# One more FFT batch transposed through DRAM, half of a batch's low parts moved to GpSimd, and its last stage two iterations sooner

## The chip, the cores and the metric

The kernel runs on one core of a Trainium2 chip. The metric is the device time of one execution in microseconds (us): the median of the runs shown. Five engines work side by side, each through its own queue of instructions in order: PE (TensorE: matmuls; PEld is its weight load), DVE (VectorE), ACT (ScalarE), POOL (GpSimd) and SP (SyncE, which here only issues DMAs). ACT issues DMAs too.

## The reference

```python
X = np.fft.rfft(x, axis=1)                       # x: 8 batches of 3136 x 256, float32
y = np.fft.irfft(X * F, n=x.shape[1], axis=1)    # F = filt_r + 1j * filt_i
h = np.maximum(y @ w_in, 0.0)                    # w_in: 256 x 1024
conv_out = sum(conv_w[k] * shift(h, k) for k in range(3))
out = (h * gate(conv_out)) @ w_out               # gate: sigmoid; w_out: 1024 x 256
```

## The kernel before, in words

The FFT over 3136 = 112 x 28 is done with matmuls, in stages. For each of 8 batches there are 14 steps (p = 0 to 13) of each stage:

- `load` (L314) brings two columns of x, 224 KB, into one of XBUFS = 7 buffers; SP issues it.
- `first` (L319) is the transform of length 112 on PE. `keep` (L333) empties its PSUM tile on ACT. For most batches it goes into an SBUF tile `turn`, which `turn` (L347, PE transposes of L352) and `turned_rows` (L355, a copy on ACT, L357) later bring into the order of the next stage. For the batches in `THROUGH_DRAM` (L577: 2, 4 and 6) `first` has another shape (L325 instead of L330), ACT writes the result to `a_dram` (L337), and `load_rows` (L341) reads it back in the new order (L344), so that PE and ACT have no transposing to do.
- `second` (L361 to L368) is the transform of length 28 on PE; `filt` (L370) multiplies by the filter with three DVE operations (L376 to L378) and adds with one on POOL (L380), giving `z`.
- `third` (L231) is the first inverse stage on PE (L234); `store` (L236) copies it on ACT (L238) and ACT writes it to `b_dram` (L240).
- `last_load` (L197) reads `b_dram` back into one of four tiles `br`; `last_stage` (L210) is the last inverse stage, eight passes of PE in L216; `last_out` (L219) splits the result into y = high + low: ACT rounds to the high part (L146), DVE subtracts to get the low part (L149). Both write y with a stride.

A loop over iterations i (L404) runs these as a pipeline, one step of each stage in each iteration: `first` of step i-1, `turn` of step m = i-17, `second` of m-1, `filt` of m-2, `third` of m-4. It ends with i = 130. In the last iterations, from 113 (`done`), there is no `first` left; batch 7 goes through its later stages, and batch 0's last stage runs beside it: its load of piece c/2 is written in iteration 115 + c/2, its matmuls one iteration later and its `last_out` two later (`LATE` = 2 in L426).

Then the feed-forward network (FFN) starts, with m counting its pieces (L550): `inner` (L476, six matmuls in L177 to L179), `relu` and scaling on ACT, `conv` on DVE (L494, L495), sigmoid on ACT (L499), product on DVE (L500), a split of g into high (ACT) and low (POOL, L152), and `project` on PE (L520 to L522), six pieces later. The first `inner` reads y of batch 0 in all 28 columns, so it waits for the last `last_out`. The last three `third` of batch 7 and their `store` run in pieces 1 to 3 of the FFN. Batches 1 to 7 have their last stages inside the FFN.

The order of the work on PE, DVE, ACT and POOL is the order in which the code is written (`manual_schedule`, L403). SP is not among these: a scheduler orders its DMA issues, in which each waits for its buffer to be free. Tiles of `a` (ABUFS = 4 buffers) serve `keep`, `load_rows` and `turned_rows`.

In the profiled execution iteration 112 starts at 299.3 us, 113 at 302.0, 115 at 305.9 and 129 at 347.7; the FFN's first matmul starts at 353.8.

Of the kernel before, what the change touches and what calls it, by code (L numbers as in the profile page):

```python
# [9 lines left out]
F32 = mybir.dt.float32  # L10
# [3 lines left out]
AF = mybir.ActivationFunctionType  # L14
# [3 lines left out]
N1 = 112  # L18
N2 = 28
G = 28  # L20
D = 256
FF = 1024
KT = D // 128
# [101 lines left out]
def tile_fft_filter_gated_ffn(  # L125
# [16 lines left out]
    nc = tc.nc  # L142
    B = x.shape[0]

    def hi_act(dst, src):
        nc.scalar.activation(dst, src, AF.Copy)  # L146

    def lo_dve(dst, src, hi):
        nc.vector.tensor_tensor(out=dst, in0=src, in1=hi.bitcast(F32), op=ALU.subtract)  # L149

    def lo_pool(dst, src, hi):
        nc.gpsimd.tensor_tensor(out=dst, in0=src, in1=hi.bitcast(F32), op=ALU.subtract)  # L152

    def to_f32(dst, raw, e, m):


        v = nc.vector
        pairs = raw.rearrange("p (n t) -> p n t", t=2)
        low, high = pairs[:, :, 0].bitcast(U32), pairs[:, :, 1]
        v.tensor_scalar(e, high, 3, 0x3FFFFFF8, op0=ALU.logical_shift_left, op1=ALU.bitwise_and)  # L160
        yield
        v.tensor_scalar(m, high, 30, 30, op0=ALU.logical_shift_right, op1=ALU.logical_shift_left)
        yield
        v.tensor_tensor(out=e, in0=e, in1=m, op=ALU.bitwise_or)
        yield
        v.tensor_scalar(m, high, 27, 0xF, op0=ALU.logical_shift_right, op1=ALU.bitwise_and)
        yield
        v.scalar_tensor_tensor(out=dst, in0=m, scalar=7.0, in1=e.bitcast(F32), op0=ALU.is_ge, op1=ALU.mult)
        yield
        v.tensor_scalar(e, dst.bitcast(I32), 23, 23, op0=ALU.logical_shift_right, op1=ALU.logical_shift_left)  # L170
        yield
        v.scalar_tensor_tensor(out=e.bitcast(F32), in0=low, scalar=2.0**-52, in1=e.bitcast(F32), op0=ALU.mult, op1=ALU.mult)
        yield
        nc.gpsimd.tensor_tensor(out=dst, in0=dst, in1=e.bitcast(F32), op=ALU.add)
# [6 lines left out]
    dram = ctx.enter_context(tc.tile_pool(name="dram", bufs=1, space=bass.MemoryType.DRAM))  # L181
    a_dram = {b: dram.tile([N2, 112, D], F32, name=f"a_dram{b}") for b in THROUGH_DRAM}
    b_dram = [dram.tile([N2, 112, D], F32, name=f"b_dram{b}") for b in range(B)]
# [18 lines left out]
    def y_slices(b, sl):  # L202
        if sl.start == 0:
            ys[b] = [yps[b % 2].tile([128, KT, S + 2], F32R, name=f"y{h}") for h in range(2)]
            for t in ys[b]:
                nc.gpsimd.memset(t[:, :, 0:1].bitcast(F32), 0.0)
                nc.gpsimd.memset(t[:, :, S + 1:S + 2].bitcast(F32), 0.0)
        return (t[:, :, 1:S + 1].rearrange("p k (a c) -> p k c a", c=N2)[:, :, sl] for t in ys[b])
# [10 lines left out]
    def last_out(b, c):  # L219
        yh, yl = y_slices(b, slice(c, c + 2))  # L220
        pv = lasts.pop((b, c))[:, 0:4 * N1].rearrange("p (k c a) -> p k c a", c=2, a=N1)
        hi_act(yh, pv)
        lo_dve(yl, pv, yh)

    NP = 14
    rest = ctx.enter_context(tc.tile_pool(name="rest", bufs=3))
# [19 lines left out]
    with (  # L246
# [4 lines left out]
        cv = convert_pools.enter_context(tc.tile_pool(name="cv", bufs=2))  # L251
# [12 lines left out]
        rows = {}  # L264
        turned_by = {b: n + 1 for n, b in enumerate(b for b in range(B) if b not in THROUGH_DRAM)}

# [27 lines left out]
        def convert_weights():  # L294

            for k in range(8):
                raw = raws.pop(k)
                em = cv.tile([128, 2, 512], I32, name="em", bufs=1)
                ws = cv.tile([128, 2, 256], F32, name="ws")
                yield from to_f32(ws.rearrange("p t n -> p (t n)"), raw.rearrange("p t n -> p (t n)"), em[:, 0], em[:, 1])  # L300
                yield
                parts = [[t.rearrange("p a b -> p (a b)")[:, 256 * k:256 * k + 256] for t in w] for w in (wi, wo)]
                for part, (wh, wl) in enumerate(parts):
                    hi_act(wh, ws[:, part])
                yield
                for part, (wh, wl) in enumerate(parts):
                    lo_pool(wl, ws[:, part], wh)
                yield
                if k < 6:
                    load_weights(k + 2)  # L310
# [3 lines left out]
        def load(b, p):  # L314
            r = xp.tile([112, 2, D], F32, name="x", bufs=XBUFS)
            nc.sync.dma_start(out=r, in_=x[b].rearrange("(p n) d -> p n d", n=N2)[:, 2 * p:2 * p + 2])
            rows["x", b, p] = r

        def first(b, p):  # L319

            r = rows.pop(("x", b, p))
            if b in THROUGH_DRAM:
                ps = fps.tile([112, 2, D], F32, name="ps")
# [8 lines left out]

        def keep(b, p, ps):  # L333
            if b in THROUGH_DRAM:
                r = fp.tile([112, 2, D], F32, name="a", bufs=ABUFS)
                nc.scalar.activation(r, ps, AF.Copy)
                nc.scalar.dma_start(out=a_dram[b][2 * p:2 * p + 2].rearrange("n p d -> p n d"), in_=r)  # L337
            else:
                nc.scalar.activation(turns[turned_by[b] % 2][:, :, 2 * p:2 * p + 2], ps, AF.Copy)
# [43 lines left out]
        def at(i):  # L383
            return divmod(i, NP) if 0 <= i < NP * B else None

        XBUFS = 7
        ABUFS = 4
        SKEW = NP + 3
        LATE = SKEW - NP - 1
# [6 lines left out]

        for i in range(XBUFS):
            load_first(i)
        csteps, wsteps = convert_conv(), convert_weights()
        done = NP * B + 1  # L400
        NI = done + LATE + N2 // 2 + 2
        END = NP * B - 4
        with tc.manual_schedule(engines=COMPUTE):  # L403
            for i in range(NI):  # L404
                m = i - SKEW
                if i == done:
                    assert next(wsteps, None) is None
                    convert_pools.close()
                    forward_pools.close()
                    yps.append(ctx.enter_context(tc.tile_pool(name="y_even", bufs=1, side="right", reuse_waits="tile")))  # L410
                    lp = ctx.enter_context(tc.tile_pool(name="lp", bufs=2, side="right", reuse_waits="tile"))
                if i:
                    load_first(i + XBUFS - 1)
                if i == 8:
                    nc.sync.dma_start(out=eye_sb, in_=eye)
                    nc.sync.dma_start(out=s2_sb, in_=s2[:, 0:120])
                    raws["cw"] = cv.tile([128, 6 * NF], I32, name="rawc", bufs=1)
                    nc.sync.dma_start(out=raws["cw"], in_=conv_w)
                if 12 <= i < 12 + NP:
                    load_filter(i - 12)  # L420
                if (bp := at(m + 2)) and bp[0] in THROUGH_DRAM:
                    load_rows(*bp)
                if i == 16:
                    nc.sync.dma_start(out=s2s_sb, in_=s2s[:, 0:120])
                    nc.sync.dma_start(out=m2_sb, in_=m2)
                c = 2 * (i - done - LATE)  # L426
                if 0 <= c - 4 < N2:
                    last_out(0, c - 4)
                if 0 <= c - 2 < N2:
                    last_stage(0, c - 2, fps.tile([128, 512], F32, name="ps"))  # L430
                if bp := at(m - 2):
                    filt(*bp)
                pt = None
                if (bp := at(m - 4)) and m - 4 <= END:
                    pt = fps.tile([112, 2, D], F32, name="ps")
                    third(*bp, pt)
                pf = first(*bp) if (bp := at(i - 1)) else None
                if bp := at(m - 1):
                    second(*bp)
                pa = turn(*bp) if (bp := at(m)) and bp[0] not in THROUGH_DRAM else None  # L440
                if pt is not None:
                    store(*at(m - 4), pt)
                if pf is not None:
                    keep(*at(i - 1), pf)
                if pa is not None:
                    turned_rows(*at(m), pa)
                if 0 <= m - 1 < NP:
                    copy_filter(m - 1)
                if 14 <= i < 22:
                    next(csteps, None)  # L450
                if i in (30, 32):
                    load_weights((i - 30) // 2)
                if i >= 36:
                    for _ in range(2 if i % 8 == 0 else 1):
                        next(wsteps, None)
                if 0 <= c < N2:
                    last_load(0, c)
# [116 lines left out]
                evacuate(*a)  # L574


THROUGH_DRAM = (2, 4, 6)  # L577
PLAG = 6
PAUSE = (8,)
AVOID = (3, 4, 5, 6, 7)  # L580
# [39 lines left out]
```

## Time and profile before

| What | us |
|---|---|
| Median of three runs (lowest, highest) | 1546.46 (1546.35, 1547.85) |
| The profiled execution | 1546.79 |
| its span in the trace | 1545.0 |
| one iteration of batch 6 without `turn` (PE) | 2.61 |
| one iteration of batch 7 with `turn` and batch 0's last stage (PE) | 3.05 |
| idle of PE ahead of the FFN | 3.31 |

The span is the time between the first and the last instruction of the trace; 1.8 us lie around it. A row of the timeline gives the start, the duration, the engine, the line and operation, what it writes and reads, and in brackets the idle time of the engine ahead of it with what ended it. PE's matmuls overlap, so the time from start to start counts, not the duration. A float32 matmul stands in the trace as two, so x4 is two matmuls. ACTq and SPq are issues of DMAs.

### The profile page before, as it was taken

The numbers are of one execution on the slowest core, as the hardware profiler recorded it, in microseconds if no ns is written. First come the engines' busy times: TensorE is split into PE (matmuls) and PEld (weight loads), VectorE is DVE, ScalarE is ACT, GpSimd is POOL, SyncE is SP. The second block draws the span as 40 slices with busy tenths as digits, with TensorE's granted clock in tenths as the row PEclk, the third lists the DMA queues.
The fourth block names the chain that finished last, engine by engine and source line by source line (L and its number), as shares of the span: only waits on it lengthen the run. The fifth ranks groups of instructions, "written<-read, shape, count | busy, mean of one in ns | idle before, by whom it ended". The sixth has DMA issues, their size and how long they took to land.

```text
span 1545.0 us, 27319 instructions
## 1 busy us (share of the span) xinstructions
PE 1520.4 (98%) x9984; PEld 1390.8 (90%) x9984; DVE 1295.3 (84%) x1978; ACT 1222.2 (79%) x2232; POOL 704.2 (46%) x625
## 2 busy tenths in 40 slices
PE   8999999998999999999999999999999999999998
PEld 7676777777999999999999999999999999999998
DVE  3879898897888888888888888888888888888887
ACT  5654646467888888888888888888888888888887
POOL 3455666543444444444444444444444444444444
PEclk9999999999999999999999999999999999999999
DMA  9888888751111011111111111111011111000001
GB/s 234 273 271 258 255 273 244 228 151 49 49 49 34 28 49 51 48 47 49 48 37 43 45 39 44 49 49 43 31 49 49 49 49 48 26 25 25 25 25 49
DMA packets 104518, 134.49 MB, mean 87 GB/s; under 512 B 8744, under 2 KB 70920, under 8 KB 104384
## 3 DMA queue, kind: packets, MB, share of 16 engines
q1 hardware_dynamic: 79968, 97.41, 20.7%
q10 hardware_dynamic: 24416, 35.33, 7.5%
q8 instruction: 80, 1.31, 0.4%
q14 instruction: 54, 0.44, 0.1%
HBM read 71.69 MB, written 61.01 MB: 86 GB/s over the span
## 4 chain that ended last, share of the span: by engine, by line
PE 93%; DVE 2%; DMA 2%; ACT 2%; issue 0%; POOL 0%; ACTq 0%; SPq 0%; POOLq 0%; DVEq 0%
PE ps_h L178 12%; PE ps_h L179 12%; PE ps_h L177 12%; PE po L520 11%; PE po L522 11%; PE po L521 11%; PE ps_h L216 6%; PE ps L234 5%; PE pp L364 5%; PE ps L330 3%; PE ps L325 2%; PE ps L352 2%; DMA x<-in_x 1%; PE ps L216 1%; DVE y L149 1%; DVE v L378 0%
## 5 line engine op out<-in xcount | busy, mean ns | idle before, releaser
L152 POOL TENSOR_TENSOR g<-t,g 128x448 fp32r<-128x448 f32 x448 | 517.9, 1156 | 662.9 <-ACT g L146 259.4
L520 PE MATMUL po<-wo,g 128*128 128x256 f32 x1568 | 441.4, 282 | 0.0
L522 PE MATMUL po<-wo,g 128*128 128x256 f32 x1568 | 433.9, 277 | 0.5 <-POOL g L152 0.5
L521 PE MATMUL po<-wo,g 128*128 128x256 f32 x1568 | 433.4, 276 | 0.0
L494 DVE SCALAR_TENSOR_TENSOR t<-ps_h,cw,t 128x448 f32<-128x448 f32 x448 | 305.6, 682 | 84.4 <-ACT t L489 73.7
L177 PE MATMUL ps_h<-y,wi 128*128 128x450 f32 x896 | 328.9, 367 | 5.5 <-DVE y L149 3.3
L178 PE MATMUL ps_h<-y,wi 128*128 128x450 f32 x896 | 330.2, 368 | 3.9 <-DVE y L149 3.9
L179 PE MATMUL ps_h<-y,wi 128*128 128x450 f32 x896 | 328.8, 367 | 0.0
L495 DVE SCALAR_TENSOR_TENSOR t<-ps_h,cw,t 128x448 f32<-128x448 f32 x448 | 306.5, 684 | 16.0
L489 ACT ACTIVATE t<-ps_h,cw 128x448 f32<-128x448 f32 x448 | 285.2, 637 | 41.8 <-ACT ps_h L487 0.7
L520 PEld LDWEIGHTS po<-wo,g 128*128 128x128 f32 x1568 | 294.8, 188 | 7.1
L521 PEld LDWEIGHTS po<-wo,g 128*128 128x128 f32 x1568 | 294.3, 188 | 5.7
L522 PEld LDWEIGHTS po<-wo,g 128*128 128x128 f32 x1568 | 294.5, 188 | 0.6 <-POOL g L152 0.6
L487 ACT ACTIVATE ps_h<-ps_h 128x450 f32<-128x450 f32 x448 | 251.8, 562 | 33.1 <-PE ps_h L179 27.2
L500 DVE TENSOR_TENSOR t<-ps_h,t 128x448 f32<-128x448 f32 x448 | 275.4, 615 | 0.1
L499 ACT ACTIVATE t<-t 128x448 f32<-128x448 f32 x448 | 255.0, 569 | 12.0 <-DVE t L495 10.9
L146 ACT ACTIVATE g<-t 128x448 fp32r<-128x448 f32 x448 | 254.5, 568 | 0.2 <-DVE t L500 0.2
L380 POOL TENSOR_TENSOR z<-u,v 120x512 f32<-120x512 f32 x112 | 157.1, 1403 | 170.9 <-DVE v L378 140.3
L177 PEld LDWEIGHTS ps_h<-y,wi 128*128 128x128 f32 x896 | 169.9, 190 | 13.9 <-DVE y L149 3.7
L179 PEld LDWEIGHTS ps_h<-y,wi 128*128 128x128 f32 x896 | 168.3, 188 | 13.9
L178 PEld LDWEIGHTS ps_h<-y,wi 128*128 128x128 f32 x896 | 168.2, 188 | 12.7 <-DVE y L149 5.9
L149 DVE TENSOR_TENSOR y<-ps_h,y 128x448 fp32r<-128x448 f32 x98 | 103.2, 1053 | 77.0 <-ACT y L146 77.0
(65 smaller groups left out, 1578.7 us busy)
## 6 DMA issues: line engine op xcount, KB each, us to landing
x<-in_x SPq DMA_DIRECT2D x112, 224.0 KB
b_dram<-sb ACTq DMA_DIRECT2D x112, 224.0 KB
br<-b_dram SPq DMA_DIRECT2D x112, 224.0 KB
out<-ot SPq DMA_DIRECT2D x27, 896.0 KB
a_dram<-a ACTq DMA_DIRECT2D x42, 224.0 KB
a<-a_dram SPq DMA_DIRECT2D x42, 224.0 KB
raw<-in_w_in SPq DMA_DIRECT2D x8, 256.0 KB
raw<-in_w_out SPq DMA_DIRECT2D x8, 256.0 KB
```

Of the source, the lines that this page charges most:

```text
L152: nc.gpsimd.tensor_tensor(out=dst, in0=src, in1=hi.bitcast(F32), op=ALU.subtract)
L177: nc.tensor.matmul(ps, lhsT=wh, rhs=rh, start=start, stop=False, **kw)
L178: nc.tensor.matmul(ps, lhsT=wh, rhs=rl, start=False, stop=False, **kw)
L179: nc.tensor.matmul(ps, lhsT=wl, rhs=rh, start=False, stop=stop, **kw)
L489: nc.scalar.activation(t, h[:, 1:SUB + 1], AF.Copy, scale=cw[:, 1, f:f + 1])
L494: nc.vector.scalar_tensor_tensor(out=t, in0=h[:, 0:SUB], scalar=cw[:, 0, f:f + 1], in1=t, op0=ALU.mult, op1=ALU.add)
L495: nc.vector.scalar_tensor_tensor(out=t, in0=h[:, 2:SUB + 2], scalar=cw[:, 2, f:f + 1], in1=t, op0=ALU.mult, op1=ALU.add)
L499: nc.scalar.activation(t, t, AF.Sigmoid)
L500: nc.vector.tensor_mul(t, h[:, 1:SUB + 1], t)
L520: nc.tensor.matmul(o, lhsT=gh[:, sl], rhs=wo[0][:, f], start=first, stop=False, skip_group_check=True)
L521: nc.tensor.matmul(o, lhsT=gh[:, sl], rhs=wo[1][:, f], start=False, stop=False, skip_group_check=True)
L522: nc.tensor.matmul(o, lhsT=gl[:, sl], rhs=wo[0][:, f], start=False, stop=last, skip_group_check=True)
```

## The change

Batch 7 joins `THROUGH_DRAM`. `keep` writes from buffers of its own, `ao`, two of them (the default of that pool), and no longer shares the four of `a`. Half of batch 0's fourteen low parts (c = 0, 4, ..., 24) are made by POOL: as POOL cannot read PSUM here, ACT first makes a second, float32 copy `yt` in SBUF. Batch 0's last stage is written two iterations sooner: load in 113 + c/2, matmuls one later, `last_out` two later, so that the last is in iteration 128. To make room, x has six buffers and the converted weights `ws` one.

```diff
@@ last_out
         hi_act(yh, pv)
-        lo_dve(yl, pv, yh)
+        if b == 0 and c % 4 == 0:
+            t = lp.tile([128, KT, 2, N1], F32, name="yt")
+            nc.scalar.activation(t, pv, AF.Copy)
+            lo_pool(yl, t, yh)
+        else:
+            lo_dve(yl, pv, yh)
@@ convert_weights
-                ws = cv.tile([128, 2, 256], F32, name="ws")
+                ws = cv.tile([128, 2, 256], F32, name="ws", bufs=1)
@@ keep
-                r = fp.tile([112, 2, D], F32, name="a", bufs=ABUFS)
+                r = fp.tile([112, 2, D], F32, name="ao")
@@ the loop
-        XBUFS = 7
+        XBUFS = 6
-                c = 2 * (i - done - LATE)
+                c = 2 * (i - done)
@@
-THROUGH_DRAM = (2, 4, 6)
+THROUGH_DRAM = (2, 4, 6, 7)
```

Lines behind L223 stand five or more further down in the changed kernel (L344 becomes L349, L234 becomes L239, L364 becomes L369).

On SP, the order of the loads at the end of the loop before. `a_dram_59` is batch 6, `b_dram_60` batch 0, `b_dram_61` batch 1:

```order
L344 DMA a<-a_dram_59 112x512
L316 DMA x<-in_x 112x512
L344 DMA a<-a_dram_59 112x512 x7
L199 DMA br<-b_dram_60 112x2x256 x14
L199 DMA br<-b_dram_61 112x2x256 x9
```

And now. `a_dram_59` is still batch 6, `a_dram_60` is batch 7, `b_dram_61` is batch 0:

```order
L349 DMA a<-a_dram_59 112x512
L199 DMA br<-b_dram_61 112x2x256 x3
L349 DMA a<-a_dram_59 112x512
L199 DMA br<-b_dram_61 112x2x256
L349 DMA a<-a_dram_59 112x512 x4
L199 DMA br<-b_dram_61 112x2x256 x2
L349 DMA a<-a_dram_60 112x512 x4
L199 DMA br<-b_dram_61 112x2x256
L349 DMA a<-a_dram_60 112x512
L199 DMA br<-b_dram_61 112x2x256
```

The first four loads of `br` now stand among batch 6's, and the fifth and sixth ahead of the first four rows of batch 7; from there a load of `br` and one of batch 7 take turns.

On PE, two iterations near the start of the tail before (L216 is batch 0's last stage, L234 `third`, L364 `second`, L352 the transposes of `turn`):

```order
L216 MATMUL ps<-m_sb,br 128x112 x4
L234 MATMUL ps<-z,i_sb 112x256 x2
L364 MATMUL pp<-a,s_sb 120x512
L352 MATMUL ps<-eye_sb,turn_101 112x128 x4
L216 MATMUL ps<-m_sb,br 128x112 x4
```

And now, from the last `first` (L330 of the changed kernel) on; L372 is the split `second` that ends batch 6:

```order
L330 MATMUL ps<-x,s_sb 112x256 x2
L369 MATMUL pp<-a,s_sb 120x512
L239 MATMUL ps<-z,i_sb 112x256 x2
L369 MATMUL pp<-a,s_sb 120x512
L216 MATMUL ps<-m_sb,br 128x112 x4
L239 MATMUL ps<-z,i_sb 112x256 x2
L369 MATMUL pp<-a,s_sb 120x512
L216 MATMUL ps<-m_sb,br 128x112 x4
L239 MATMUL ps<-z,i_sb 112x256 x2
L372 MATMUL pp<-a,s_sb 120x256
```

The transposes are gone, and batch 0's last stage begins one iteration behind the last `first`, while batch 6 is still in `second`.

On DVE, the tail before (L149 the low part, the rest `filt`):

```order
L149 TENSOR_TENSOR y_3115<-ps,y_3114 128x2x2x112
L376 TENSOR_TENSOR u<-pp,t_sb 120x512
L377 TENSOR_TENSOR v_105<-pp,t_sb 56x512
L378 TENSOR_TENSOR v_105<-pp,t_sb 56x512
L149 TENSOR_TENSOR y_3115<-ps,y_3114 128x2x2x112
```

And now:

```order
L149 TENSOR_TENSOR y_3079<-ps,y_3078 128x2x2x112
L381 TENSOR_TENSOR u<-pp,t_sb 120x512
L382 TENSOR_TENSOR v_107<-pp,t_sb 56x512
L383 TENSOR_TENSOR v_107<-pp,t_sb 56x512
L381 TENSOR_TENSOR u<-pp,t_sb 120x512
L382 TENSOR_TENSOR v_106<-pp,t_sb 56x512
L383 TENSOR_TENSOR v_106<-pp,t_sb 56x512
L149 TENSOR_TENSOR y_3079<-ps,y_3078 128x2x2x112
```

DVE now has one low part in two iterations instead of one in each. On POOL the other low parts stand ahead of the addition of `filt` in every second iteration; on ACT the copy `yt` stands between the high part and `store`.

## The prediction

> **What bounds the kernel now.** I read the page first, then the timelines of PE, DVE and ACT from the last `first` into the FFN, then the windows of DMA and clock. The page:
>
> ```profile
> PE 1520.4 (98%) x9984; PEld 1390.8 (90%) x9984; DVE 1295.3 (84%) x1978; ACT 1222.2 (79%) x2232; POOL 704.2 (46%) x625
> ...
> DMA  9888888751111011111111111111011111000001
> ```
>
> PE is busy for 98% of the span, so time is to be had only from PE's work or its few gaps; DMA is dense only up to about 300 us. PE's timeline, iterations 112 to 115, then the last of the tail:
>
> ```profile
> 299.34 1.03 PE L234 MATMUL ps<-z,i_sb 120*112 120x256 f32 x4
> 300.20 1.04 PE L330 MATMUL ps<-s_sb,x 112*128 112x112 f32 x8
> 301.08 1.03 PE L364 MATMUL pp<-a,s_sb 112*120 112x512 f32 x2
> 301.95 1.03 PE L234 MATMUL ps<-z,i_sb 120*112 120x256 f32 x4
> 302.82 1.02 PE L364 MATMUL pp<-a,s_sb 112*120 112x512 f32 x2
> 303.68 1.03 PE L234 MATMUL ps<-z,i_sb 120*112 120x256 f32 x4
> ...
> 305.85 1.12 PE L234 MATMUL ps<-z,i_sb 120*112 120x256 f32 x4 [0.28 <-POOL z L380]
> ...
> 344.66 1.04 PE L216 MATMUL ps<-m_sb,br 112*128 112x112 f32 x8
> 345.54 1.03 PE L234 MATMUL ps<-z,i_sb 120*112 120x256 f32 x4
> 346.41 1.02 PE L364 MATMUL pp<-a,s_sb 112*120 112x512 f32 x2
> 347.27 0.60 PE L352 MATMUL ps<-eye_sb,turn 128*112 128x128 f32 x4
> 347.71 1.04 PE L216 MATMUL ps<-m_sb,br 112*128 112x112 f32 x8
> ...
> 349.89 0.59 PE L367 MATMUL pp<-a,s2s_sb 112*120 112x256 f32 x2
> 353.80 0.48 PE L177 MATMUL ps_h<-y,wi 128*128 128x450 f32 x1 [3.31 <-DVE y L149]
> ```
>
> From start to start an iteration of the tail takes 3.05 us: 0.88 for L216, 0.87 for L234, 0.86 for L364, 0.44 for the transposes. Without these it is 2.61, as in iteration 112. At the end PE waits 3.31 us for y. DVE keeps just the same pace:
>
> ```profile
> 302.22 0.69 DVE L376 TENSOR_TENSOR u<-pp,t_sb 120x512 f32<-120x512 f32 x1 [0.48 <-PE pp L364]
> ...
> 312.87 0.99 DVE L149 TENSOR_TENSOR y<-ps,y 128x448 fp32r<-128x448 f32 x1 [2.03 <-ACT y L146]
> 313.76 0.69 DVE L376 TENSOR_TENSOR u<-pp,t_sb 120x512 f32<-120x512 f32 x1
> ...
> 315.92 1.00 DVE L149 TENSOR_TENSOR y<-ps,y 128x448 fp32r<-128x448 f32 x1
> ...
> 352.77 0.97 DVE L149 TENSOR_TENSOR y<-ps,y 128x448 fp32r<-128x448 f32 x1
> ...
> 355.08 0.69 DVE L378 TENSOR_TENSOR v<-pp,t_sb 56x512 f32<-56x512 f32 x1
> 356.88 0.68 DVE L494 SCALAR_TENSOR_TENSOR t<-ps_h,cw,t 128x448 f32<-128x448 f32 x1 [1.11 <-ACT t L489]
> ```
>
> A low part costs DVE 0.89 (312.87 to 313.76), a `filt` 2.16 (313.76 to 315.92), 3.05 together, with no idle time. So PE's transposes alone are worth nothing in the tail: DVE would hold the pace. The three parts of the change belong together. ACT has room:
>
> ```profile
> 349.65 0.60 ACT L238 ACTIVATE sb<-ps 112x512 f32<-112x512 f32 x1 [0.26 <-PE ps L234]
> 350.28 0.31 ACTq L240 DMA_DIRECT2D b_dram<-sb  x1
> 350.64 0.99 ACT L146 ACTIVATE y<-ps 128x448 fp32r<-128x448 f32 x1 [0.39 <-ACT sb L238]
> ```
>
> ```profile
> 358.98 0.60 ACT L238 ACTIVATE sb<-po 112x512 f32<-112x512 f32 x1 [2.13 <-PE po L234]
> ...
> 361.06 0.57 ACT L499 ACTIVATE t<-t 128x448 f32<-128x448 f32 x1
> ```
>
> **The change part by part.** *PE.* Fourteen times 0.44 = 6.2 us of transposes go, and the 0.28 wait of iteration 115 goes too, since `last_stage` now fills that place. PE's new schedule from 301.95: iteration 113 takes 1.73 (301.95 to 303.68), iterations 114 to 127 take 14 x 2.61 = 36.6, iterations 128 and 129 (no `last_stage`) 1.73 each: free at 343.8, where it now is at 350.3.
>
> *DVE.* Its first low part is c = 2 in iteration 116. Following the order on ACT: 115 starts at 306.3 and its `third` ends 0.88 + 1.03 later, at 308.2; `store` and its issue take 1.0 (349.65 to 350.64), the high part 1.0, so DVE starts at 310.25. From there it has 7 low parts and the `filt` of iterations 116 to 130: 7 x 0.89 + 15 x 2.16 = 38.6, nothing between them if PE and ACT stay ahead. Its pair of iterations takes 5.21, PE's 5.22: matched again. The last low part (iteration 128) ends three `filt` before the end of that chain, at 342.4, ahead of PE's 343.8: the wait of 3.31 goes. The chain's end is 348.9.
>
> *POOL and ACT.* These rows price what they gain:
>
> ```profile
> L152 POOL TENSOR_TENSOR g<-t,g 128x448 fp32r<-128x448 f32 x448 | 517.9, 1156 | 662.9 <-ACT g L146 259.4 <-issue 244.4 <-POOL g L152 83.7
> ...
> L500 DVE TENSOR_TENSOR t<-ps_h,t 128x448 f32<-128x448 f32 x448 | 275.4, 615 | 0.1
> ...
> L339 ACT ACTIVATE turn<-ps 128x448 f32<-128x448 f32 x70 | 38.1, 544 | 33.9 <-PE ps L330 30.6 <-ACT sb L238 3.2
> ```
>
> ```profile
> L380 POOL TENSOR_TENSOR z<-u,v 120x512 f32<-120x512 f32 x18 | 23.1, 1283 | 30.4 <-DVE v L378 18.8 <-PE ps L234 10.7 <-PE pp L364 0.9
> ```
>
> ACT loses 14 copies of `turned_rows` and gains 7 `yt` of 0.54: less work. A low part on POOL has no row with strides. Below, L152's 1.16; above, L152 times the 1.6 by which DVE's strided low part (1.00) exceeds its contiguous product (L500), about 1.9. I take 1.4. A pair on POOL is then 2 x 1.28 + 1.4 = 4.0, and even 4.5 fits into 5.2. Queued behind it is `z` of the same iteration, for which `third` waits two iterations later. In 117, POOL is free at 314.6 (DVE's `filt` of 116 ends at 313.3, then 1.28); at 1.16 `z` ends at 317.0, at 1.9 at 317.8, and `third` of 119 wants it at 317.6: once 0.2 late at worst. The Trainium skill, GPSIMD Engine Reference, section "Performance pitfalls for Q7 kernels", says that reading SBUF at a step over 8 bytes costs half as much again; yh is read at 112 bytes, so by it 1.7 us, an estimate, and `z` would come just as it is needed, with the sum higher by 0 to 0.1. No row of this trace has that form.
>
> *The start of the FFN.* PE's start is 10.0 us sooner. At the old start the clock fell, too:
>
> ```profile
> 354.00:359.00 5.00, 5.00 (x18) 4.33 (x18) 3.08 (x5) 1.18 (x3) 1.47 (x2) 0.66 0.00 0
> ```
>
> The third number from the end is the granted clock: 0.66 over these 5.00 us, so 1.7 us are lost. Without the long gap that goes. But not all 11.7 is kept: DVE's chain now ends at 348.9, behind PE's start, and `conv` of the first piece stands behind it. Two `conv` operations take 1.40 (356.88 to the end of the second), so the first sigmoid on ACT starts at 350.3 instead of 361.06; the copies ahead of it on ACT are done by then (`store` of 358.98 moves to 347 or 348). From the first sigmoid on, the order is unchanged: 10.7 us are kept.
>
> *SP.* In the new order the loads of `br` stand four pieces ahead, the fifth and sixth before batch 7's first rows. The first of these is therefore issued only after `last_stage` of iteration 115 (307.3) and one more issue: about 307.7, and `second` of iteration 116 needs it at 310.7, so 3.0 us to land. The later ones have four iterations. Landing times on the chain that ended last:
>
> ```profile
> 18.04 4.64 DMA x<-in_x
> ...
> 71.07 6.06 DMA raw<-in_w_in
> ```
>
> These are from a loaded stage; here three transfers overlap. Late by 0 to 1.7; I take 0.3, part of it under DVE's chain.
>
> *DMA in iterations 99 to 112.* Each now carries batch 7's write besides batch 6's read, `b_dram`, and until 106 x: four times 229,376 bytes in 2.61 us, 351 GB/s.
>
> ```profile
> 212.00:219.00 7.00, 7.00 (x40) 5.33 (x39) 6.54 (x11) 3.26 (x6) 5.38 (x5) 1.00 1.02 359
> 266.00:274.00 8.00, 8.00 (x48) 6.45 (x48) 6.66 (x11) 4.19 (x8) 4.43 (x3) 1.00 0.83 252
> ```
>
> The last column is GB/s. 359 has been carried for 7 us with PE busy throughout; 252 is what this place carries now. x can be late by five iterations, so I put it at nothing, with the bound below. `ws` and six x buffers: the weights' next use comes several iterations later, and six tiles of x are still 15 us ahead of PE; at nothing. Batch 7's `first` costs PE the same in its other shape (L330 takes 0.88, L234, of the same size as the other shape, 0.87).
>
> Sum: -10.7 + 0.3 = -10.4 against the profiled execution's 1546.79: **1536.4**. The median of the runs is 0.3 lower than that execution; I leave that in the range.
>
> **The rivals.** *DMA becomes the bound in iterations 99 to 106.* If it carries 300 instead of 351 GB/s, an iteration takes 3.06 and eight of them lose 3.6: 1540.0; at 270, 3.40 and 6.3: 1542.7. For it: that demand is 2% under the highest window. Against: that window itself, and the slack of x. The Trainium skill, DMA: Bandwidth & Descriptors, section "Where 436 GB/s comes from", puts the HBM side at about 358 GB/s; by it the demand just fits, and the 359 of the trace agrees. Chance 0.15.
>
> *The ring of two `ao` holds ACT (slower).* A buffer is filled (0.60), issued (0.36) and must land before it is used two iterations later: an iteration takes at least (0.96 + landing)/2. At 4.26 us that is 2.61, no loss; with the 6.06 above it is 3.51, and 14 iterations lose 12.6: 1549.0; at 6.7, 3.83 and 17.1: 1553.5. It turns slower from a landing of 6.2 us on. Queued behind ACT's wait are `store` and the next `keep`, so PE runs out of PSUM tiles. For it: these iterations carry the most traffic. Against: batches 2, 4 and 6 already use each `a` after two iterations, and ACT waited little there:
>
> ```profile
> ACT a L336 <- DMA x<-in_x: 1.5, 3, 0.6
> ```
>
> Chance 0.05.
>
> *POOL becomes the bound instead of DVE, so that the tail's pace does not fall as the change says.* From a low part of 2.65 us on, POOL's pair exceeds 5.21; at 4 us seven pairs lose 9.5: 1545.9, no change. For it: the strided form is unmeasured. Against: 2.65 is 2.3 times L152. Chance 0.06.
>
> **How the numbers follow.** The forecast has 0.74. No change means within 0.2%, 3.1 us, about what a measurement of this kernel can tell. Low end: all of PE's 11.7 kept and 0.3 of the median, 1534.8. High end: DMA at about 270 GB/s, 1542.7. Left out are the other rivals' 0.11 and little else. Faster: 0.74 + 0.15 = 0.89; same 0.06; slower 0.05.
>
> **What would show it.** Right: no L352 for batch 7, L216 to L216 in 2.61 us, 14 L149 of batch 0 become 7, the first L177 near 343.8 with no wait for y and a clock of 1.00, and the first sigmoid near 350.3. Wrong: a POOL low part over 2.65 us; waits of PE for `a` (L369) beyond 0.5 us or for `br`; waits of ACT for DMAs near its `ao` copies; iterations 99 to 106 longer than 2.61; or idle time on DVE in the tail, which would mean that its chain is not what I take it for.

## The result, and the profile after

| | runs | median us | ratio to the kernel before, 95% interval |
|---|---|---|---|
| before | 4 | 1547.15 (1546.35 to 1548.01) | |
| changed | 4 | 1537.25 (1536.85 to 1537.78) | 0.9936 (0.9919 to 0.9953) |
| the changed kernel a second time, beside other runs of before (median 1547.91) | 4 | 1538.47 (1537.06 to 1540.03) | 0.9945 (0.9928 to 0.9961) |

The profiled execution of the changed kernel took 1537.1 us with a span of 1535.3, against 1546.79 and 1545.0 before: 9.7 us less. 1536.4 was predicted. The interval excludes no change. In an experiment further down one run of five took 6815.7 us; no profile covers it, and it is left out there.

In the page after, PE's busy time is 8.4 us lower (1520.4 to 1512.0), and DMA stays dense for longer, 9 and 8 in the eighth and ninth slice where it had 7 and 5:

```profile
PE 1512.0 (98%) x9872; PEld 1381.0 (90%) x9872; DVE 1287.5 (84%) x1971; ACT 1218.3 (79%) x2225; POOL 712.0 (46%) x632
...
DMA  9888887981111111111101111111011111000001
```

PE's timeline after, from the last `first` (L330) to the FFN's first matmul (L177). Columns: start, duration, engine and line, operation, and in brackets the idle time ahead of it with who ended it. Line numbers are 5 higher than before from `third` on: L239 is `third`, L369 and L372 `second`, L216 the last stage.

```profile
299.78 1.03 PE L330 MATMUL ps<-x,s_sb 112*112 112x256 f32 x4
300.64 1.02 PE L369 MATMUL pp<-a,s_sb 112*120 112x512 f32 x2
301.50 1.03 PE L239 MATMUL ps<-z,i_sb 120*112 120x256 f32 x4
...
311.00 1.09 PE L369 MATMUL pp<-a,s_sb 112*120 112x512 f32 x2 [0.65 <-DMA a<-a_dram]
311.92 1.04 PE L216 MATMUL ps<-m_sb,br 112*128 112x112 f32 x8
...
314.53 1.04 PE L216 MATMUL ps<-m_sb,br 112*128 112x112 f32 x8
...
341.42 1.12 PE L239 MATMUL ps<-z,i_sb 120*112 120x256 f32 x4 [0.67 <-POOL z L385]
...
344.00 1.12 PE L239 MATMUL ps<-z,i_sb 120*112 120x256 f32 x4 [0.60 <-POOL z L385]
...
345.63 0.55 PE L177 MATMUL ps_h<-y,wi 128*128 128x450 f32 x1
```

Three things: from L216 to L216 it is 2.61 us where it was 3.05; L177 follows without a wait, where PE waited 3.31 us for y; and there are three waits that were not there before, one for batch 7's first row from DRAM, two for `z` near the end.

DVE's timeline after, its first low parts (L149), the last, and the start of the FFN's `conv` (L499):

```profile
309.79 0.98 DVE L149 TENSOR_TENSOR y<-ps,y 128x448 fp32r<-128x448 f32 x1 [1.56 <-ACT y L146]
...
315.90 0.99 DVE L149 TENSOR_TENSOR y<-ps,y 128x448 fp32r<-128x448 f32 x1 [0.94 <-ACT y L146]
...
321.12 1.02 DVE L149 TENSOR_TENSOR y<-ps,y 128x448 fp32r<-128x448 f32 x1
...
342.12 1.03 DVE L149 TENSOR_TENSOR y<-ps,y 128x448 fp32r<-128x448 f32 x1
...
349.53 0.68 DVE L499 SCALAR_TENSOR_TENSOR t<-ps_h,cw,t 128x448 f32<-128x448 f32 x1
```

A pair of iterations takes 5.22 (315.90 to 321.12). The one gap in the chain is the 0.94 us at 315.90: the high part on ACT stands behind `store`, and `store` behind a `third` that PE started late because of the missing row. On ACT, the issue of batch 7's last write (L342; ACTq rows are ACT's issues of DMAs), and much later the way to the first sigmoid (L504; it was at 361.06):

```profile
303.40 0.32 ACTq L342 DMA_DIRECT2D a_dram<-ao  x1
...
349.32 0.60 ACT L243 ACTIVATE sb<-po 112x512 f32<-112x512 f32 x1 [0.54 <-PE po L239]
...
350.31 0.53 ACT L492 ACTIVATE ps_h<-ps_h 128x450 f32<-128x450 f32 x1 [0.39 <-ACT sb L243]
350.87 0.63 ACT L494 ACTIVATE t<-ps_h,cw 128x448 f32<-128x448 f32 x1
351.40 0.57 ACT L504 ACTIVATE t<-t 128x448 f32<-128x448 f32 x1
```

**Where the time came from.** From the first sigmoid to the end it is 1545.0 - 361.06 = 1183.9 us before and 1535.3 - 351.40 = 1183.9 after, and in every experiment below it is 1183.8 to 1184.0. So all of the change lies ahead of that point. It can be split at the `third` of iteration 113, which follows the last `first` by two instructions (301.95 before, 301.50 after): 0.45 us come from the part ahead of it, and 9.21 from the **stretch** from there to the first sigmoid, 59.11 before and 49.90 after. The part ahead differs from profile to profile by more than that, as the table below shows; that it came out within 0.5 us here is luck. So the experiments are read by the stretch, and their medians only beside it.

### The profile page after: what moved, and what is told of

It is laid out like the page before. It is cut to its first block, busy times and chain, and to the rows that moved or that the text cites. A ratio compares the mean times of both kernels' runs of the same rounds, so it can differ in the third digit from the quotient of the medians.

```text
span 1535.3 us, 27151 instructions
## 1 busy us (share of the span) xinstructions
PE 1512.0 (98%) x9872; PEld 1381.0 (90%) x9872; DVE 1287.5 (84%) x1971; ACT 1218.3 (79%) x2225; POOL 712.0 (46%) x632
## 4 chain that ended last, share of the span: by engine, by line
PE 91%; DVE 3%; DMA 3%; ACT 2%; issue 1%; POOL 1%; ACTq 0%; SPq 0%; POOLq 0%; DVEq 0%
PE ps_h L178 12%; PE ps_h L179 12%; PE ps_h L177 12%; PE po L525 11%; PE po L527 11%; PE po L526 11%; PE ps_h L216 6%; PE ps L239 5%; PE pp L369 4%; PE ps L330 3%; PE ps L335 2%; PE ps L357 1%; DMA x<-in_x 1%; DVE y L149 1%; DMA t_sb<-in_fi 1%; DVE v L383 1%
## 5 line engine op out<-in xcount | busy, mean ns | idle before, releaser
L499 DVE SCALAR_TENSOR_TENSOR t<-ps_h,cw,t 128x448 f32<-128x448 f32 x448 | 305.5, 682 | 81.4 <-ACT t L494 70.9
L177 PE MATMUL ps_h<-y,wi 128*128 128x450 f32 x896 | 328.6, 367 | 2.1 <-DVE t L505 1.9
L504 ACT ACTIVATE t<-t 128x448 f32<-128x448 f32 x448 | 255.0, 569 | 11.8 <-DVE t L500 10.7
L177 PEld LDWEIGHTS ps_h<-y,wi 128*128 128x128 f32 x896 | 169.6, 189 | 10.1 <-DVE t L505 2.9
L149 DVE TENSOR_TENSOR y<-ps_h,y 128x448 fp32r<-128x448 f32 x98 | 103.2, 1053 | 76.9 <-ACT y L146 76.9
```

The source lines that it names most:

```text
L177: nc.tensor.matmul(ps, lhsT=wh, rhs=rh, start=start, stop=False, **kw)
L499: nc.vector.scalar_tensor_tensor(out=t, in0=h[:, 0:SUB], scalar=cw[:, 0, f:f + 1], in1=t, op0=ALU.mult, op1=ALU.add)
L504: nc.scalar.activation(t, t, AF.Sigmoid)
```

## The experiments

The theory was that in the tail PE (3.05 us per iteration) and DVE (3.05) go at the same pace, so that relieving one alone gains next to nothing there; the two-iteration move closes the hole ahead of the FFN. The rival was that each part is worth its own share and the shares add up. Six kernels have one or two of the three parts; all of them keep the other edits (own `ao` buffers, six for x, one `ws`), which the row of the kernel before does not have. "D" is batch 7 through DRAM, "P" half of the low parts on POOL, "S" the last stage sooner. What they undo of the changed kernel:

```diff
-THROUGH_DRAM = (2, 4, 6, 7)
+THROUGH_DRAM = (2, 4, 6)                  # without D
-        if b == 0 and c % 4 == 0:
+        if False:                          # without P
-                c = 2 * (i - done)
+                c = 2 * (i - done - LATE)  # without S
```

| parts | start of the stretch | first sigmoid | stretch us | median us (runs) | ratio, 95% interval |
|---|---|---|---|---|---|
| none (before) | 301.95 | 361.06 | 59.11 | | |
| D | 299.94 | 358.56 | 58.62 | 1546.13 (10) | 0.9991 (0.9982 to 1.0001) |
| S | 303.25 | 358.08 | 54.83 | 1543.28 (5) | 0.9964 (0.9951 to 0.9977) |
| P | 302.92 | 359.42 | 56.50 | 1546.38 (10) | 0.9996 (0.9986 to 1.0005) |
| D, S | 300.30 | 355.16 | 54.86 | 1542.51 (4) | 0.9958 (0.9943 to 0.9973) |
| D, P | 302.61 | 354.65 | 52.04 | 1540.53 (4) | 0.9946 (0.9931 to 0.9961) |
| P, S | 304.08 | 358.61 | 54.53 | 1542.82 (10) | 0.9972 (0.9963 to 0.9981) |
| D, P, S (changed) | 301.50 | 351.40 | 49.90 | 1537.25 (4) | 0.9936 (0.9919 to 0.9953) |
| D, P, S, second time | 300.68 | 351.38 | 50.70 | 1538.47 (4) | 0.9945 (0.9928 to 0.9961) |

Start and sigmoid are read from the timelines of PE and ACT in one profile each. The start scatters by 4 us, between 299.94 and 304.08. That blurs the medians: P alone is 1.5 us under its own runs of before by median and 2.6 shorter in the stretch. The stretch scatters too. In three profiles with the changed kernel's schedule (the third has three `ao` buffers, below) it is 49.90, 50.70 and 50.28, while the sigmoid comes at 351.40, 351.38 and 351.29: what PE gains ahead of the stretch it waits longer for batch 7's first row. Differences under 0.8 us between stretches are therefore not told apart.

**D alone.**

> Batch 7 goes through DRAM (with the changed kernel's buffers), but all 14 low parts of batch 0 stay on DVE and its last stage comes as late as before. Theory (DVE holds the tail at 3.05 us an iteration, so PE's transposes alone are worth next to nothing): DVE's first low part starts some 1.5 us sooner (311.4 instead of 312.87) because iteration 115 has no transposes, and all else is as before: 1545 to 1547 us, L216 to L216 still about 3.05 us, and PE waits within the tail. Rival (the parts add up: PE is the bound and the 6.2 us of transposes are gained by themselves): 1541 us, L216 to L216 at 2.61.

PE's timeline in the tail of this kernel:

```profile
325.99 1.04 PE L216 MATMUL ps<-m_sb,br 112*128 112x112 f32 x8
327.24 1.12 PE L239 MATMUL ps<-z,i_sb 120*112 120x256 f32 x4 [0.21 <-POOL z L385]
328.19 1.02 PE L369 MATMUL pp<-a,s_sb 112*120 112x512 f32 x2
329.05 1.04 PE L216 MATMUL ps<-m_sb,br 112*128 112x112 f32 x8
```

The transposes are gone and, once PE has caught up with DVE, the iteration still takes 3.06: PE now waits for `z`, which stands behind DVE's chain. The 6.2 us of PE's work are worth 0.5 in the stretch. The theory holds, the sum of shares does not.

**S alone.**

> Batch 0's last stage two iterations sooner; no batch 7 through DRAM, all 14 low parts on DVE. Theory: work per iteration is unchanged (3.05 on PE and DVE), y is ready before PE asks, so the wait of 3.31 and the clock loss of 1.7 go, but DVE's three filters behind the last low part hold the first conv back: DVE's chain ends near 355 instead of 355.8, first sigmoid near 356.5 instead of 361.1: 1542.5 us, 4.5 less than before. Rival (parts add up: what the whole change brings beyond the 6.2 of transposes): 1543.5 us. This run tells the two apart only together with the next.

The stretch is 4.3 shorter. PE keeps its 3.05, and goes into the FFN with no wait for y (3.31 before), and the clock does not fall there:

```profile
341.10 1.04 PE L216 MATMUL ps<-m_sb,br 112*128 112x112 f32 x8
344.14 1.04 PE L216 MATMUL ps<-m_sb,br 112*128 112x112 f32 x8
...
352.31 0.55 PE L177 MATMUL ps_h<-y,wi 128*128 128x450 f32 x1
```

**D and S.**

> The whole change but for POOL: all 14 low parts on DVE. Theory: DVE has 18 filters of 2.16 and 14 low parts of 0.89 from 302 on and some 1.5 us idle, so its chain ends near 355 whatever PE has shed, first sigmoid near 356: 1542 us, the same as with the last stage sooner alone within 1 us. Rival (parts add up): 6 us less than that run, 1537 us, the same as the changed kernel.

54.86 against 54.83 with S alone: next to S, D is worth nothing. Its L216 at 325.07, 328.13 and 331.20 have the same 3.06 with a wait for `z` of 0.21 in each iteration.

**D and P.**

> Batch 7 through DRAM and half of the low parts on POOL, but batch 0's last stage as late as before. Theory: the tail's pace falls to 2.61 (14 x 0.44 = 6.2 us), but y is again ready only in iteration 130, so PE waits about 3 us ahead of the first L177 and the clock falls to 0.5 for some 4 us: first L177 near 347.5, 1541 us. Rival (POOL's share is worth nothing, parts add up): the same time as the run with DRAM alone, 1541 in both.

```profile
347.40 0.64 PE L177 MATMUL ps_h<-y,wi 128*128 128x450 f32 x1 [2.38 <-DVE y L149]
```

With both engines relieved the stretch falls by 7.1 us: next to P, D is worth 4.5 (56.50 to 52.04). What S then takes away is this wait of 2.38 us and the slow clock behind it (7.25 us from L177 to the sigmoid instead of 5.77); as it brings waits of its own, for batch 7's first row and for `z`, it comes to 2.1.

**P and S**, and **P alone.**

> Half of the low parts on POOL and the last stage two iterations sooner, but batch 7 still turned by PE. Theory: PE's 3.05 us per iteration set the tail; 41.7 + 14 x 0.44 = 47.9 us from iteration 113's third to the first L177 and 5.8 to the first sigmoid, 53.7, against 54.83 of the sooner start alone: 1541.5 to 1542.5. Rival, that the parts add: POOL is worth what it gave beside the DRAM (58.62 - 52.04 = 6.6 us), so 48.2 us in that stretch and about 1536.7.

> Half of the low parts on POOL alone: batch 7 turned by PE, the last stage at its old place. Theory: PE sets the tail with 3.05 us per iteration as before; only the wait for y at the end gets shorter, by about 0.9 us (2.38 instead of 3.31, as with the DRAM beside it): 57.5 to 58.5 us from iteration 113's third to the first sigmoid instead of 59.1, and 1545.5 to 1546.5. Rival, that the parts add: 52.5 us in that stretch and 1540.5.

P next to S is worth 0.3 us (54.83 to 54.53), where 1.1 was expected and the rival had 6.6; PE's pace stays at 3.05 (L216 at 341.93 and 344.98). The first sigmoid comes 6.21 us after L177 (352.40 to 358.61) where PE's order alone gives 5.77: on DVE three `filt` still stand ahead of `conv`. P alone is worth 2.6 in the stretch, more than the 0.6 to 1.6 of the theory and far from the rival's 6.6. PE's wait for y is 2.26 instead of 3.31, so 1.05 less, where about 0.9 was expected; not expected was the clock:

```profile
353.71 0.47 PE L177 MATMUL ps_h<-y,wi 128*128 128x450 f32 x1 [2.26 <-DVE y L149]
```

```profile
353.00:357.00 4.00, 3.29 (x17) 2.96 (x17) 3.16 (x5) 1.16 (x2) 2.54 (x3) 1.00 0.01 3
```

The granted clock (third number from the end) is 1.00 behind this wait, where it was 0.66 behind the 3.31 of before; L177 to the sigmoid takes 5.71 instead of 7.26. Those 1.55 are the rest. Had the clock fallen here too, the stretch would be about 58.05, an estimate, and D next to P worth 6.0, nearly all of PE's 6.2. In the D, P kernel the clock was 0.57 in the 4 us behind the wait of 2.38. Two waits for x near 70 us go the other way round: 1.89 us with a clock of 0.61 behind it (the kernel with all low parts on POOL), 2.23 us with 1.00 (the changed kernel). So in this range the length of the wait alone does not decide whether the clock falls; what does stays open.

**The changed kernel again**, beside the next three.

> The changed kernel once more, on the same chip as the next three: 1537 us. Both theories the same.

1538.47 us; its stretch is 0.8 longer, since its wait for batch 7's first row is 1.43 instead of 0.65; the row's matmul (310.96) and the sigmoid (351.38) come when they came before.

**All 14 low parts on POOL.** DVE then has only `filt`, 2.16 us per iteration, and PE alone sets the pace.

> All 14 low parts of batch 0 on POOL, not 7. Theory (in the changed kernel DVE's chain, equal to PE's pace, is what delays the last two additions by 0.67 and 0.60 us and the first conv): DVE keeps only its filters, PE's waits for z at the end of the tail go, and PE's first L177 comes about 1.5 to 2 us sooner after the tail's start; POOL needs 1.28 + 1.37 = 2.65 by durations but some 2.6 from start to start, just PE's pace: 1535.5 us. Rival (POOL becomes the bound and y's last low part comes late): waits of PE for z in every iteration and a wait for y from POOL ahead of L177, 1537 to 1540 us.

```diff
-        if b == 0 and c % 4 == 0:
+        if b == 0:
```

1538.68 us (4 runs), ratio 0.9940 (0.9923 to 0.9958): no better than the changed kernel, and its stretch is 51.62. PE's timeline and the window of the clock:

```profile
302.13 1.03 PE L239 MATMUL ps<-z,i_sb 120*112 120x256 f32 x4
...
313.26 1.91 PE L369 MATMUL pp<-a,s_sb 112*120 112x512 f32 x2 [2.28 <-DMA a<-a_dram]
314.96 1.89 PE L216 MATMUL ps<-m_sb,br 112*128 112x112 f32 x8
316.64 1.11 PE L239 MATMUL ps<-z,i_sb 120*112 120x256 f32 x4
...
347.97 0.55 PE L177 MATMUL ps_h<-y,wi 128*128 128x450 f32 x1
```

```profile
313.00:317.00 4.00, 3.74 (x12) 2.69 (x13) 1.66 (x3) 0.95 (x2) 2.96 (x3) 0.57 0.85 283
```

After 316.64 PE never waits again for `z` or y; its pace is 2.60. The theory's 1535.5 did not come. The time is the rival's, but its mechanism is not there, since PE waits for nothing from POOL. At 313.26, though, PE had waited 2.28 us for batch 7's first row, and the clock fell to 0.57 over the next 4 us, 1.7 us more. What DVE's relief brought was lost at the start of the tail.

**One `ao` buffer, and three.** These test the rival of the two-buffer ring.

```diff
-                r = fp.tile([112, 2, D], F32, name="ao")
+                r = fp.tile([112, 2, D], F32, name="ao", bufs=1)   # or bufs=3, with XBUFS = 5
```

> The changed kernel with one buffer ao instead of two. Theory (the ring holds ACT at 0.96 + landing per iteration once that exceeds PE's pace): with landings of 3.0 to 4.4 an iteration of batches 2, 4, 6 and 7 takes 4.0 to 5.3 instead of 3.05 or 2.61, together 50 to 80 us: 1585 to 1615 us. Rival (PSUM tiles and the other queues hide the ring): 1537 to 1545 us.

> The changed kernel with three buffers ao (and five of x, to make room). Theory (ACT's waits for ao, 9.3 us in ten places, are hidden: PE does not wait for ACT there): the waits go and the time stays, 1537 us within 1 us. Rival (the ring of two costs PE something in batch 7): 1534 to 1536 us.

One buffer: 1585.15 us in its single run. ACT's timeline in iterations that write batch 7:

```profile
280.10 0.60 ACT L341 ACTIVATE ao<-ps 112x512 f32<-112x512 f32 x1 [1.50 <-DMA a_dram<-ao]
...
283.15 0.60 ACT L341 ACTIVATE ao<-ps 112x512 f32<-112x512 f32 x1 [0.97 <-DMA a_dram<-ao]
...
286.54 0.60 ACT L341 ACTIVATE ao<-ps 112x512 f32<-112x512 f32 x1 [1.31 <-DMA a_dram<-ao]
...
289.99 0.60 ACT L341 ACTIVATE ao<-ps 112x512 f32<-112x512 f32 x1 [0.77 <-DMA a_dram<-ao]
```

In these rows an iteration takes 3.05 to 3.45 us, which is the 0.96 of filling and issue and a landing of 2.1 to 2.5 us, shorter than the 3.0 to 4.4 expected. So the mechanism is real. With two buffers ACT waits as well, but PE is not held by it, and three buffers take the waits for `a_dram<-ao` away without a gain: 1538.12 us (1536.99 to 1540.63), ratio 0.9941 (0.9926 to 0.9957), stretch 50.28. From the waits of the changed kernel (in total, times, longest):

```profile
ACT ao L341 <- DMA a_dram<-ao: 9.3, 10, 1.9
```

**The first row of batch 7 sooner.** Batch 7's first `a` row gathers from every row that `first` wrote, so it can be read only once the write of iteration 112 has landed. In the changed kernel that is not all: SP's order puts the read behind the sixth load of `br`, which waits for PE's last stage of iteration 115 and is issued at 306.90:

```profile
304.30 2.92 SPq L199 DMA_DIRECT2D br<-b_dram  x2
307.39 1.98 SPq L349 DMA_DIRECT2D a<-a_dram  x4
```

The next two kernels move that write ahead of a `store` on ACT, the first of them in the changed kernel, the second in the one with all low parts on POOL. SP's order moves with it: the first three reads of batch 7 now stand ahead of the sixth load of `br`.

```diff
+                if pf is not None and i == NP * B:
+                    keep(*at(i - 1), pf)
                 if pt is not None:
                     store(*at(m - 4), pt)
-                if pf is not None:
+                if pf is not None and i < NP * B:
                     keep(*at(i - 1), pf)
```

> The changed kernel, with one edit: in iteration 112 ACT copies and writes batch 7's last first (ao) before it stores a third, and in SP's order batch 7's first three rows (a) now stand ahead of the sixth br load. Theory: the late first a row (PE waited 0.65 us in one profile of the changed kernel, 1.43 in the other) is a real loss in the tail, because the DVE chain behind it has no slack; the wait of L369 for a is gone or under 0.3 us, and from the start of iteration 113's third to the first sigmoid it takes 49.0 to 49.4 us instead of 49.90 and 50.70: 1536.2 to 1536.8. Rival: the wait is covered by DVE's own chain, as the prediction had it for a part; then the stretch stays at 49.9 and the time at 1537.2.

1536.96 us (5 runs), ratio 0.9936 (0.9923 to 0.9948). PE's wait for the row is 0.21 us, as the theory had it, but the stretch is 50.29 (300.48 to 350.77), not 49.0 to 49.4. The read is issued 1.7 us sooner after the stretch's start (4.23 instead of 5.89), its matmul starts only 0.4 sooner (9.06 instead of 9.50): from issue to matmul it now takes 4.83 us instead of 3.61. On DVE the first low part starts no sooner:

```profile
309.88 1.00 DVE L149 TENSOR_TENSOR y<-ps,y 128x448 fp32r<-128x448 f32 x1 [2.67 <-ACT y L146]
...
315.26 1.01 DVE L149 TENSOR_TENSOR y<-ps,y 128x448 fp32r<-128x448 f32 x1 [0.18 <-ACT y L146]
```

The rows of ACT ahead of these:

```profile
305.42 1.03 ACTq L245 DMA_DIRECT2D b_dram<-sb  x1
306.50 1.00 ACT L146 ACTIVATE y<-ps 128x448 fp32r<-128x448 f32 x1 [1.11 <-issue]
...
309.63 0.64 ACT L243 ACTIVATE sb<-ps 112x512 f32<-112x512 f32 x1
311.59 0.31 ACTq L245 DMA_DIRECT2D b_dram<-sb  x1
311.94 1.01 ACT L146 ACTIVATE y<-ps 128x448 fp32r<-128x448 f32 x1 [1.67 <-DMA a<-a_dram]
```

An issue took 1.03 us instead of 0.31, and another began, by the profile, only when a read of `a` had landed. The high parts on ACT stand behind these issues, and DVE's chain behind the high parts. The theory, that the late row by itself is what the chain loses, is not borne out by this kernel: with the row nearly in time, the same chain is held by ACT's issues. This is one profile. A long issue of ACT stands in the kernel before as well (1.09 us at 248.75), so that the edit or its traffic made these two slow is not shown.

> All 14 low parts of batch 0 on POOL, and the same edit of iteration 112 as in the run beside it. Theory: with all low parts on POOL, PE alone sets the tail, and what ate the gain in the earlier run with 14 was the late a row (2.28 us) and the clock that fell behind it (two instructions of 1.9 us instead of 1.0). With the row in time, PE's own work is left: 1.73 + 14 x 2.61 + 2 x 1.73 = 41.7 us from iteration 113's third to the first L177, 5.8 more to the first sigmoid, 47.5 instead of 49.9: about 1534.9. Rival: the row is late again (its landing, not its place in the queues, decides), 51 to 52 us in that stretch: 1538 to 1539.

The four comparable runs took 1534.8 to 1538.74 us, median 1536.3; ratio 0.9931 (0.9917 to 0.9944).

```profile
301.02 1.03 PE L239 MATMUL ps<-z,i_sb 120*112 120x256 f32 x4
...
310.81 1.09 PE L369 MATMUL pp<-a,s_sb 112*120 112x512 f32 x2 [0.94 <-DMA a<-a_dram]
```

The wait is 0.94 instead of 2.28 us, and no instruction behind it is slow. The stretch is 48.61 (301.02 to 349.63, where ACT's first sigmoid starts), 3.01 less than with all low parts on POOL alone; the wait (1.34) and the clock (1.7) make 3.04. Without the 0.94 it would be 47.7, against the theory's 47.5. This kernel has the shortest stretch, by 1.3 us against the changed kernel's 49.90; its measured time is not apart from the changed kernel's, whose interval overlaps with this one's. A gain over the changed kernel is therefore seen in one profile's stretch only.

## Why the prediction was right, point by point

- **PE's pace: right.** 2.61 per iteration of the tail. PE reached L177 at 345.63, not 343.8 (the terms as put add up to 343.7). By its own work it was to take 41.85 from the stretch's start and took 44.13. Of these 2.28, 0.65 is the wait for batch 7's first row, 1.27 the two waits for `z`, and the rest lies around these waits, where a matmul takes 1.09 or 1.12 instead of 1.02 or 1.03 and its overlap with the one before is lost. The two waits for `z` were not foreseen: in the last iterations without a last stage PE needs 1.73 us, less than the 2.16 of a `filt` on DVE, so it catches up with DVE's chain.
- **DVE's chain: right in its length, but not free of gaps.** Its first low part was put at 310.25 and came at 309.79; the pair takes 5.22 as against 5.21; the last low part was to end at 342.4 and ended at 343.15. The chain's end was put at 348.9 and is 349.53: it began 0.46 sooner and lost 0.94 us to the gap that the late row caused through ACT.
- **That the parts belong together: right for D and P, not for S.** D is worth 0.5 alone and 0.0 beside S, but 4.5 beside P and 4.6 beside P and S. S pays without the others: 4.3 alone, 2.1 beside D and P, since P takes part of the same wait ahead of the FFN.
- **POOL's low part: right.** It was put at 1.4, between 1.16 and 1.9. The group after:

```profile
L152 POOL TENSOR_TENSOR g<-t,g 128x448 fp32r<-128x448 f32 x448 | 517.2, 1155 | 660.2 <-ACT g L146 256.8 <-issue 247.0 <-POOL g L152 81.9
...
L152 POOL TENSOR_TENSOR y<-yt,y 128x448 fp32r<-128x448 f32 x7 | 9.7, 1383 | 0.0
```

  1.383 against 1.155 without strides is 1.20 times, not the half more of the Trainium skill's GPSIMD Engine Reference, section "Performance pitfalls for Q7 kernels"; the measurement decides.
- **The start of the FFN: right in kind, 1.1 us late.** The wait of 3.31 is gone, and the clock is 1.00 (first row below). The first sigmoid came at 351.40 instead of 350.3. It was put 1.4 us behind DVE's chain; `conv` was done at 350.94, and what came last was PE's and ACT's order. ACT's `store`, put at 347 or 348, waited for PE's `third` at the start of the FFN (0.54, 349.32), since PE was late, and two instructions of the second piece follow it ahead of the sigmoid. From L177 it is 5.77 us where 6.5 was put (343.8 to 350.3), and 5.8 in the other kernels that enter the FFN without a wait, except the one with P and S.
- **SP and the first row of batch 7: the term that was mis-sized.** It was put at 0 to 1.7 us late, taken at 0.3 with a part hidden. The issue was right (307.39 where about 307.7 was put); the landing was not: the matmul started 3.61 us behind the issue, and in other kernels 4.4 to 4.8, where 3.0 were taken as the time to spare. Measured are waits of 0.65 and 1.43 in two profiles of the changed kernel, and 2.28 with a fall of the clock where DVE had been relieved further. In the changed kernel it is not hidden, since it delays DVE's chain through ACT; but taking most of it away made the stretch no shorter there (50.29, against 49.90 and 50.70), so what it costs that kernel by itself stays open. With all low parts on POOL, it and the clock behind it cost 3.0.
- **DMA: right.** In windows of the changed kernel (last column GB/s, third from the end the clock):

```profile
344.00:349.00 5.00, 5.00 (x25) 4.40 (x25) 4.78 (x8) 1.76 (x3) 2.58 (x2) 1.00 0.31 93
...
266.00:274.00 8.00, 8.00 (x39) 6.05 (x38) 6.71 (x11) 4.22 (x8) 4.54 (x3) 1.00 0.95 301
274.00:287.00 13.00, 13.00 (x52) 8.93 (x51) 12.19 (x19) 6.24 (x12) 8.21 (x6) 1.00 0.98 328
287.00:302.00 15.00, 15.00 (x59) 10.19 (x59) 11.91 (x18) 6.58 (x12) 8.53 (x9) 1.00 1.02 338
```

  301 GB/s is the rival's rate, and its consequence, 3.06 us per iteration, did not come: PE is busy throughout in the last three windows, and from the last `first` of batch 6 to the last of batch 7 it took 37.82 us where it took 38.12 before. The rival failed in its step from the rate to the pace. That `x` can come some iterations late without being missed, as the prediction argued, fits this; no run here shows which transfer lagged.
- **The two-buffer ring: rightly held unlikely.** One buffer shows its mechanism, three that at two it costs no more than the scatter. **POOL as the bound** did not come either: 1.383 us is far from 2.65.

The sum had 10.7 us kept at the first sigmoid, less 0.3 for the row: 10.4. Measured are 9.66 at the sigmoid and 9.7 in the execution. The 0.7 too much come out as follows: PE's stretch to L177 took 2.28 more than put, it began 0.45 sooner, and L177 to the sigmoid took 0.73 less, 1.1 in all at the sigmoid, of which 0.3 had been taken for the row. So two misses partly cancel, and the sooner start is scatter: the total is closer than its terms. Three signs that the prediction named for being wrong did show, each of them small: PE waited 0.65 us for `a` (0.5 was the bound), ACT waited for DMAs at its `ao` copies, and DVE stood idle for 0.94 us in the tail.

## What to carry to other kernels

Where two engines go at the same pace, taking work from one shows as little and taking it from both as much; read the pace of each engine in the stage before pricing a cut. Data that goes out to DRAM and comes back transposed is complete only when its last piece has landed: find the first reader behind the last writer, and give it that time, since what is relieved elsewhere is lost there. Compare variants by the stretch between two fixed points in the trace when the rest of the program scatters by more than the effect, and take several profiles of one kernel first, to see how far the stretch itself scatters.

## What the hardware showed that was not expected

- From the issue of the last write of batch 7 to the start of the matmul that needs its first row it took 7.6 us in the changed kernel (303.40 to 311.00). In the kernel with all low parts on POOL it took 9.0 (304.25 to 313.26). This is no pure round trip, since SP issues the sixth load of `br` in between. In the D, P kernel, where the read waits for nothing but the write, it was issued 2.6 us behind the write's issue (303.86 to 306.49), and its matmul started 3.6 us later, without a wait.
- Near the start of the tail an issue on ACT's queue took up to 1.65 us instead of 0.31 (305.31 in the kernel with all low parts on POOL; 1.03 in the rows of ACT above), and one began, by the profile, only when another queue's read had landed.
- A `first` in the shape that goes through DRAM makes an iteration of 2.59 us with `second` and `third` where the other shape makes 2.61; over 14 iterations that is the 0.3 us by which the forward part ended sooner beside its scatter.
- Behind waits of PE near 2 us the clock over the next 4 us was 0.57 (after 2.28 and 2.38), 0.61 (after 1.89) or 1.00 (after 2.23 and 2.26).
